# One fetch of the turned probabilities per pair of groups, a plan that counts open transfers, and two PSUM tiles for the last sums

## The chip, the cores and the metric

The kernel runs on one core of a Trainium2 chip. TensorE (PE) multiplies matrices, VectorE (DVE), ScalarE (ACT) and GpSimd (POOL) work on elements, and SyncE (SP) issues every transfer (DMA) of this kernel. The metric is the device time of one execution in microseconds (us); lower is better. The three runs of the kernel before took 588.96, 589.66 and 590.10 us, with a median of 589.66.

## The reference

An attention over four batches of eight heads and 768 positions feeds a feed-forward layer. Each query sees the keys less than 16 positions away, and beside them one summary for each of the 24 blocks of 32 keys: the block's largest key, element by element, and its mean value. All arrays are fp32.

```python
def _attn_ref(q, k, v):                       # B, H, S, D = 4, 8, 768, 64
    k_sum = k.reshape(B, H, nb, block, D).max(axis=3)        # block = 32, nb = 24
    v_sum = v.reshape(B, H, nb, block, D).mean(axis=3)
    scores_l = scale * np.matmul(q, k.transpose(0, 1, 3, 2))
    mask_l = np.abs(pos[:, None] - pos[None, :]) < window    # window = 16
    scores_s = scale * np.einsum('bhsd,bhnd->bhsn', q, k_sum) + np.log(block)
    scores_all = np.concatenate([np.where(mask_l, scores_l, -1e9), scores_s], axis=-1)
    a = softmax(scores_all)
    return np.matmul(a, np.concatenate([v, v_sum], axis=2))

x = attn_out.transpose(0, 2, 1, 3).reshape(B * S, H * D)     # 3072 x 512
out = (np.maximum(x @ w_in, 0.0) ** 2) @ w_out               # 512 -> 2048 -> 512
```

## The kernel before, in words

**Tiling.** The 3072 tokens are cut into 48 groups of 64 queries (a window of one batch, all eight heads). A window's 64 queries see 94 local keys and 24 block keys, 118 in all. Eight groups are a unit of 512 tokens, which is what the feed-forward layer works on. Every fp32 product there is made of three products of a high and a low part, so a group of six matmuls on PE (four with the high part `gh`, two with the low part `gl`, each 128x512) is the usual step. Of the six units, two are worked directly: `ffn` with the hidden product (line 1050) and the outer one (line 1074). The other four are two couples, each worked with seven products in place of eight (`first_product` line 1340, `products` line 1454, `mixed` line 1647 for the second couple's first layer with weights folded by the kernel itself). The weights `wW` come in sixteen chunks (`raw<-wW`, line 983), are split into high and low parts by ACT (line 986) and DVE (lines 989 to 1003), and stay in SBUF tiles `w...`.

**A visit.** Groups are worked in pairs. A visit of PE is the scores of one pair (line 647) followed by the values of an earlier pair (line 854). Between a pair's scores and its values lie: the mask (DVE, line 721), the exponential (ACT, line 778), the normalisation (DVE, lines 790 to 797), the turn of the probabilities from queries to keys, and the values. For the first eight groups PE turns them. From then on a group's probabilities are turned in three steps:

- T (line 826): DVE transposes each 32x32 block of a 128x512 tile into a tile `a`.
- TW (line 837): SP stores `a` in a DRAM buffer `turn`, one transfer of 256 KB.
- TR (line 841): SP fetches it back into `a` with the blocks in their new places, four transfers of 64 KB, one for each 32 partitions.

So a pair takes two stores and eight fetches. The fetches of one group wait for that group's own store.

**What sets the order.** Nothing is emitted in program order. Each piece of work is a task of the class `Plan` with an engine, an estimated cost, a sort key (mostly a due time) and the buffers that it takes and uses. `Plan.order` plays the tasks through, each engine always taking the ready task with the smallest key, and the instructions are emitted in that order. Every engine then runs its own list strictly in order: an instruction that waits holds all that are behind it on its engine. For SP this means that a load waiting for PE to free its tile holds the transfers behind it. On top of that, each transfer is given one of eight completion semaphores in turn, and waits for the transfer eight before it in SP's list. The plan before knows the rate of transfers and the engine's issue time, but not these eight. The constants at the head of the file (`VISITS`, `T0`, `STEP`, `SUMS`, `HALF_AT` and others) are the due times and leads that go into the keys.

**The tiles that the change touches.** `a` and `r`, two slots of 128x512 each, hold the turned probabilities; pairs use them in turn, except for the earliest. `turn` has four DRAM buffers of one group. In PSUM lie two double tiles `o0` and `o1` of 2x128x512, and two tiles `att0` and `att1` and two `h` of 128x512. In `products`, a couple's seven products (j from 0 to 6) are summed in PSUM, and `acc` names the tiles; products 4 and 6 share `acc[4]`, which is the double tile `o0`. The function `plus` adds such a sum to an SBUF tile on DVE (line 1400) and `leave` stores the result (line 1393). For the last product of the last couple the sum is already in two halves of 512 columns, `C12`, which both read `o0`.

## Time and profile before

| what | value |
|---|---|
| median of three runs | 589.66 us |
| profiled execution | 588.6 us |
| its span, first to last instruction or transfer | 586.8 us |
| PE busy | 573.3 us (98%) |
| DVE / ACT / POOL busy | 443.9 / 353.0 / 99.2 us |
| granted clock of PE | full throughout |
| bytes moved | 149.63 MB, mean 255 GB/s |
| SP waiting for a store `turn<-a` at a fetch | 12.0 us, 10 times |
| SP waiting for DVE at a store `turn<-a` | 20.7 us, 14 times |

Rows of a timeline read: start in us, length in us, engine, line, operation, output and input, size, and how many alike follow each other; in brackets is the engine's idle time just before and what ended it. The listed length of a matmul overlaps the next one. A row of SP is the time it took to issue, not the transfer itself. The chain of waits, followed back from the last instruction, has rows of the same kind, and there a DMA row is the time from issue to landing.

### The profile page before, as it was taken

What the parts mean: (1) busy time and instruction counts of PE and PEld (TensorE: products, weight loads), DVE (VectorE), ACT (ScalarE), POOL (GpSimd) and SP (SyncE); (2) the same over time, 40 slices, a digit from 0 to 9 for tenths busy, and PEclk for the clock granted to TensorE, in tenths of its full rate; (3) what the DMA queues carried; (4) which work ended last, traced back from release to release, by engine and by line L of the source; (5) the groups of instructions that cost most, each with busy time, mean ns of one, the idle gap of its engine ahead of it and who ended that gap; (6) DMA issues with size and microseconds to landing.
All of it is one profiled execution on the core that took longest, in us unless ns stands there. A gap on an engine that the chain in (4) does not pass through costs nothing.

```text
span 586.8 us, 12058 instructions
## 1 busy us (share of the span) xinstructions
PE 573.3 (98%) x4084; PEld 467.0 (80%) x4084; DVE 443.9 (76%) x1018; ACT 353.0 (60%) x876; POOL 99.2 (17%) x165
## 2 busy tenths in 40 slices
PE   8999999999999999999999999999999999999996
PEld 6787878777788888888778888888878888888885
DVE  5999899578457647765986877999968966769863
ACT  2999877667646646465754566676746424654442
POOL 4300005073568004420120022000000000000000
PEclk9999999999999999999999999999999999999999
DMA  8998885869998796996979945999885456667672
GB/s 313 324 394 304 304 301 161 289 214 336 356 325 261 235 332 201 322 320 185 268 248 296 363 153 183 295 303 287 271 268 178 122 158 194 197 187 232 196 225 99
DMA packets 120273, 149.63 MB, mean 255 GB/s; under 512 B 10556, under 2 KB 79164, under 8 KB 120212
## 3 DMA queue, kind: packets, MB, share of 16 engines
q1 hardware_dynamic: 120212, 148.86, 78.0%
q8 instruction: 33, 0.54, 0.4%
q14 instruction: 28, 0.23, 0.1%
HBM read 103.99 MB, written 44.04 MB: 252 GB/s over the span
## 4 chain that ended last, share of the span: by engine, by line
PE 71%; DMA 14%; DVE 5%; SPq 3%; ACT 3%; issue 2%; POOL 2%; DVEq 0%; ACTq 0%
PE o L1454 26%; PE h L1340 15%; PE o L1074 8%; PE o L1647 6%; DMA raw<-wW 6%; PE h L1050 6%; PE sz L1647 4%; PE x L854 3%; PE att L647 2%; DMA qvpa_lent<-vF 2%; DMA turn<-a 2%; DMA a<-turn 1%; PE att L1647 1%; DMA fv_lent<-vS 1%; DMA scr_i<-w 1%
## 5 line engine op out<-in xcount | busy, mean ns | idle before, releaser
L1454 PE MATMUL o<-gh,w 128*128 128x512 f32 x448 | 121.5, 393 | 0.0
L1436 ACT CAST gh<-g 128x512 fp32r<-128x512 f32 x112 | 68.5, 621 | 54.4 <-PE o L1454 25.2
L1454 PEld LDWEIGHTS o<-gh,w 128*128 128x128 f32 x448 | 83.1, 188 | 18.4 <-ACT gh L1436 0.8
L1441 DVE TENSOR_TENSOR gl<-g,gh 128x512 fp32r<-128x512 f32 x112 | 76.5, 695 | 20.9 <-ACT gh L1436 20.6
L1050 PE MATMUL h<-xh,w 128*128 128x512 f32 x240 | 75.0, 392 | 1.2 <-DVE w L1003 0.9
L1454 PE MATMUL o<-gl,w 128*128 128x512 f32 x224 | 69.5, 391 | 0.0
L1340 PE MATMUL h<-xh,w 128*128 128x512 f32 x224 | 69.1, 390 | 0.0
L1074 PE MATMUL o<-w,gh 128*128 128x512 f32 x240 | 62.2, 395 | 1.4 <-ACT gh L1061 1.2
L778 ACT ACTIVATE p<-p,small 128x118 f32<-128x118 f32 x160 | 61.0, 386 | 1.1 <-DVE small L721 0.7
L1050 PEld LDWEIGHTS h<-xh,w 128*128 128x128 f32 x240 | 44.7, 188 | 12.2 <-DVE w L1003 1.7
L1074 PEld LDWEIGHTS o<-w,gh 128*128 128x128 f32 x240 | 44.3, 188 | 11.8 <-ACT gh L1061 1.9
L1454 PEld LDWEIGHTS o<-gl,w 128*128 128x128 f32 x224 | 41.8, 188 | 9.6 <-DVE gl L1441 0.9
L1340 PEld LDWEIGHTS h<-xh,w 128*128 128x128 f32 x224 | 42.0, 188 | 9.1 <-ACT r L1350 0.4
L1050 PE MATMUL h<-xl,w 128*128 128x512 f32 x120 | 46.7, 389 | 0.0
L1340 PE MATMUL h<-xl,w 128*128 128x512 f32 x112 | 43.6, 389 | 0.0
L1350 ACT ACTIVATE r<-h 128x512 f32<-128x512 f32 x32 | 19.1, 596 | 37.1 <-PE h L1340 36.9
L660 POOL COPY kb<-kb 128x96 f32<-128x96 f32 x25 | 8.6, 343 | 193.3 <-ACT kw L672 70.9
L1064 DVE TENSOR_TENSOR gl<-r,gh 128x512 fp32r<-128x512 f32 x30 | 23.2, 774 | 20.3 <-ACT gh L1061 16.9
L721 DVE CUSTOM_DVE_ANT_0 p<-att,mask 128x118 f32<-128x118 f32 x152 | 33.1, 275 | 2.6 <-PE att L647 2.5
L1074 PE MATMUL o<-w,gl 128*128 128x512 f32 x120 | 33.6, 389 | 0.0
L1431 DVE TENSOR_TENSOR g<-g 128x512 f32<-128x512 f32 x48 | 32.8, 689 | 0.4
L778 ACT ACTIVATION_READ_ACCUMULATOR p<-p,small 128x1 f32 x160 | 30.4, 190 | 0.0
(209 smaller groups left out, 1077.7 us busy)
## 6 DMA issues: line engine op xcount, KB each, us to landing
raw<-wW SPq DMA_DIRECT2D x32, 512.0 KB
w<-scr_s SPq DMA_DIRECT2D x64, 256.0 KB
w<-scr_a SPq DMA_DIRECT2D x48, 256.0 KB
turn<-a SPq DMA_DIRECT2D x40, 256.0 KB
a<-turn SPq DMA_DIRECT2D x160, 64.0 KB
scr_t<-ci SPq DMA_DIRECT2D x32, 256.0 KB
w<-scr_i SPq DMA_DIRECT2D x32, 256.0 KB
w<-scr_t SPq DMA_DIRECT2D x32, 256.0 KB
```

The lines of the kernel that those rows point to most:

```text
L721: nc.vector.tensor_tensor_reduce(out=pr.tile[:, j, :KEYS], in0=score_at(g, 0, j), in1=mask_of(g)[0], scale=-SCALE, scalar=-NEG, op0=ALU.ad ...
L778: nc.scalar.activation(x, score_tile(g, p % parts)[:, p] if by_pe else x, AF.Exp, bias=nm.tile[:, p : p + 1], scale=SCALE if by_pe else -1 ...
L1050: nc.tensor.matmul(cut(h), lhsT=lhs.tile[:, k * P : (k + 1) * P], rhs=rhs[:, k, c0 : c0 + n], start=(i == 0), stop=(i == 3 * KT - 1),)
L1064: lambda: nc.vector.tensor_tensor(out=cut(gl), in0=cut(r), in1=cut(gh).bitcast(F32), op=ALU.subtract),
L1074: nc.tensor.matmul(o_of(o, t), lhsT=terms[i][0].tile[:, (t - t0) * P : (t - t0 + 1) * P], rhs=terms[i][1].tile, start=(first and i == 0), ...
L1340: nc.tensor.matmul(h.tile, lhsT=lhs.tile[:, k * P : (k + 1) * P], rhs=rhs[:, k, c0 : c0 + TU], start=(i == 0), stop=(i == 3 * KT - 1),)
L1350: t2 = add(f"RL{name}", "ACT", 0.56, lambda: nc.scalar.activation(r.tile, h.tile, AF.Relu), due + 2 - R_LEAD, [t1], take=[r], use=[h])
L1431: lambda x=x, ins=ins, op=op: nc.vector.tensor_tensor(out=x.tile, in0=ins[0].tile, in1=ins[1].tile, op=op),
L1436: f"GH{s}_{n}", "ACT", 0.54, lambda x=x, gh=gh: nc.scalar.copy(out=gh.tile, in_=x.tile), due - GH_LEAD, ready,
L1441: lambda x=x, gh=gh, gl=gl: nc.vector.tensor_tensor(out=gl.tile, in0=x.tile, in1=gh.tile.bitcast(F32), op=ALU.subtract),
L1454: nc.tensor.matmul(o.tile[:, d], lhsT=chunk.tile[:, w * HALF + d * P : w * HALF + (d + 1) * P], rhs=y.tile, start=begins and w == 0 and y ...
L1647: nc.tensor.matmul(o.tile, lhsT=lhs(w, k), rhs=y[k], start=begins and i == 0, stop=i == 5, skip_group_check=not begins,)
```

## The change

1. **The fetch.** The turned probabilities of a pair lie in one 128x1024 tile (one slot `a`, one slot `rr`, the same SBUF as the two of 128x512 had), and one of two DRAM buffers holds both groups of a pair. Each group is still turned and stored by itself. The fetch is a task of the pair: four transfers of 128 KB after both stores, where there were two times four of 64 KB, each four after its own store. Bytes and the 512-byte runs are the same.
2. **The plan** counts open transfers: a task says how many it issues (`issues`), and a list of the last eight landings of each queue holds an issue back until the one eight before it has landed. The assumed rate goes from 350 to 400 GB/s, and a fetch is counted as `TR_COST`.
3. **The last sums.** For the second couple, products 4 and 6 are summed in the two tiles `att0` and `att1`, held together by the small class `Banks`, and not in the double tile `o0`. The sum after product 4 (`C22`) is made in two halves.
4. **The numbers** that the plan's keys are made from are all new, so the order changes on every engine, over the whole program.

```diff
...
...
-TR_LEAD = 14
-VISITS = 52.2, 68.6, 100.8, 120.6, 146.3, 157.3, 168.5, 203.8, 235.1, 248.6, 260.4, 276.5, 297.7, 318.5, 349.1, 370.1, 390.1, 396.1, 402.1, 408.1, 416.9
+TR_COST = 1.9
+TR_LEAD = 20
+VISITS = 49.9, 82.3, 89.1, 118.5, 125.9, 145.2, 165.2, 188.4, 200.7, 237.6, 248.4, 254.4, 281.2, 289.4, 332.1, 355.6, 367.5, 379.2, 399.2, 406.4, 412.4
...
         return self.of(self.buf.tile)
 
 
+class Banks:
+
+
+    def __init__(self, bufs):
+        self.bufs = bufs
+
+    @property
+    def tile(self):
+        return self
+
+    def __getitem__(self, at):
+        d = at[1]
+        if isinstance(d, int):
+            return self.bufs[d].tile
+        assert d.stop == d.start + 1
+        return self.bufs[d.start].tile.unsqueeze(1)
+
+
-        self.take, self.use = ([getattr(b, "buf", b) for b in x] for x in (take, use))
+        self.take, self.use = ([getattr(c, "buf", c) for b in x for c in getattr(b, "bufs", (b,))] for x in (take, use))
 
 
 class Plan:
 
 
 
-    HOP, DMA_LATENCY, DMA_RATE = 0.12, 1.9, 350e3
+    HOP, DMA_LATENCY, DMA_RATE, LANES = 0.12, 1.9, 400e3, 8
 
 
 
...
     def __init__(self):
         self.tasks = []
 
-    def add(self, name, engine, cost, emit, key, after=(), take=(), use=(), size=0, begin=0.0, behind=None, late=0.0, keeps=False):
+    def add(self, name, engine, cost, emit, key, after=(), take=(), use=(), size=0, begin=0.0, behind=None, late=0.0, keeps=False, issues=1):
-        t.behind, t.late, t.keeps = behind, late, keeps
+        t.behind, t.late, t.keeps, t.issues = behind, late, keeps, issues if size else 0
         t.index = len(self.tasks)
         self.tasks.append(t)
         for b in t.take + t.use:
...
+        lanes = {}
 
...
                 t = found
                 if t is None:
                     continue
+                before = lanes.setdefault(e, [0.0] * self.LANES)
+                if t.issues and before[-self.LANES] > now:
+                    free[e] = before[-self.LANES]
+                    heapq.heappush(events, (free[e], n + 0.25, None))
+                    continue
                 tasks.remove(t)
                 for b in t.take:
                 free[e] = end = now + t.cost + self.SWITCH * (t.narrow and not narrow)
+                for i in range(1, t.issues):
+                    free[e] = end = max(end, before[i - self.LANES] + t.cost * (1 - i / t.issues))
                 if e == "PE":
                     narrow = t.narrow
                 if t.size:
                     pipe = max(pipe, end) + t.size / self.DMA_RATE
                     end = pipe + self.DMA_LATENCY + t.late
+                    before.extend([end] * t.issues)
                 t.end = end
                 n += 1
                 heapq.heappush(events, (end + self.HOP, n, t))
...
 
 
     items = [(u, f) for u in range(NU) for f in range(NF)]
-    T0, SLOW, STEP, LEAD = 28.0, 6.4, 6.2, 1.5
+    T0, SLOW, STEP, LEAD = 28.5, 6.4, 5.9, 1.5
...
         warm(i)
 
 
-    q_bufs, v_bufs, p_bufs, a_bufs = {}, {}, {}, {}
+    both_r = sb.tile([P, 2 * TU], F32, tag="rr", name="rr", bufs=1)
+    kinds["r"] = Slots(None, "r", 2, [both_r[:, k * TU : (k + 1) * TU] for k in range(2)])
+    kinds["rr"] = Slots(sb, "rr", 1)
+    kinds["a"] = Slots(sb, "a", 1)
+    q_bufs, v_bufs, p_bufs, a_bufs, both_a, both_d, t_TW = {}, {}, {}, {}, {}, {}, {}
     first_v = [x for i in range(-(-S // P // 4)) for x in lend(f"fv{i}")]
     for g in reversed(range(NG)):
         pairs = (P, NPAIR, P)
...
             q_bufs[g] = buf("q", 3, (P, NPAIR, TQ), F32, f"q{g}")
             v_bufs[g] = buf("v", NV, (P, DM), F32, f"v{g}", fixed=True)
             p_bufs[g] = buf("p", 2, pairs, F32, f"p{g}", fixed=True)
-            a_bufs[g] = buf("a" if g < APART or g // 2 % 2 == 0 else "r", 2, (P, DM), F32, f"a{g}")
+            if g % 2:
+                both_a[g // 2] = Buf(kinds["a" if g < APART or g // 2 % 2 == 0 else "rr"], (P, 2 * DM), F32, f"a{g}")
+            a_bufs[g] = Part(both_a[g // 2], g % 2 * DM, (g % 2 + 1) * DM)
 
 
     t_S, t_M, t_KC, t_T, t_V, t_XL, t_A, t_LV = ({} for _ in range(8))
...
 
             assert not early
             rest = [t_G[0, NQ - 1, k] for k in (2, 3)] if g >= APART else []
-            t_T[g] = add(f"T{g}", "DVE", 0.63, turn, due - 9, [t_n, *rest], take=[a], use=[pr])
-            d = buf("turn", 4, (NSQ, SQ, NSQ, NPAIR * SQ), F32, f"turn{g}", dr)
+            t_T[g] = add(
+                f"T{g}", "DVE", 0.63, turn, due - 9, [t_n, *rest], take=[] if g % 2 else [a], use=[pr] + [a] * (g % 2),
+                behind=t_T[g - 1] if g % 2 else None,
+            )
+            if not g % 2:
+                both_d[g // 2] = buf("turn", 2, (2, NSQ, SQ, NSQ, NPAIR * SQ), F32, f"turn{g}", dr)
+            d = both_d[g // 2]
 
             def store():
-                nc.sync.dma_start(out=d.tile.rearrange("i c j e -> (i c) (j e)"), in_=a.tile)
+                nc.sync.dma_start(out=d.tile[g % 2].rearrange("i c j e -> (i c) (j e)"), in_=a.tile)
 
             def fetch():
                 for j in range(NSQ):
                     nc.sync.dma_start(
-                        out=a.tile[j * SQ : (j + 1) * SQ].rearrange("c (i e) -> c i e", i=NSQ),
-                        in_=d.tile[:, :, j].rearrange("i c e -> c i e"),
+                        out=both_a[g // 2].tile[j * SQ : (j + 1) * SQ].rearrange("c (b e) -> c b e", e=NPAIR * SQ),
+                        in_=d.tile[:, :, :, j].rearrange("b i c e -> c (b i) e"),
                     )
 
-            t_w = add(f"TW{g}", "SP", 0.45, store, due - 8.5 - TR_LEAD, [t_T[g]], take=[d], use=[a], size=4 * P * DM, late=TURN_LATE[0])
-            t_A[g] = add(f"TR{g}", "SP", 1.75, fetch, due - 8 - TR_LEAD, [t_w], use=[a, d], size=4 * P * DM, late=TURN_LATE[1])
+            t_TW[g] = add(
+                f"TW{g}", "SP", 0.45, store, due - 8.5 - TR_LEAD, [t_T[g]], take=[] if g % 2 else [d],
+                use=[a] + [d] * (g % 2), size=4 * P * DM, late=TURN_LATE[0], behind=t_TW[g - 1] if g % 2 else None,
+            )
+            if not g % 2:
+                return
+            t_A[g - 1] = t_A[g] = add(f"TR{g}", "SP", TR_COST, fetch, due - 8 - TR_LEAD, [t_TW[g - 1], t_TW[g]], use=[a, d], size=8 * P * DM, late=TURN_LATE[1], issues=4)
 
     def values(both, x_of):
         for i, g in enumerate(both):
...
             if s:
                 sums[s][-1].update({("before", k): mixed_end[k] for k in range(2)})
         *acc, u2, u3, made = sums[s]
+        if s and len(acc) == 6:
+            acc[4:] = [Banks([Buf(kinds["atts"], None, None, f"acc{s}_{d}") for d in range(2)])]
+            sums[s] = [*acc, u2, u3, made]
         bank = acc[0], acc[1], acc[2], acc[3], acc[4], acc[3], acc[4]
 
         def by_two(x):
...
             elif j == 3:
                 last_of("w1_1", plus("U3", u3, o, u2, due, [t_p, made["U2"]], [u3]))
             elif j == 4:
-                leave(f"22_{s}", u3, 1, 1, due + 1, [plus("C22", u3, o, u3, due, [t_p, made["U3"]])])
-                made["before", 5] = [made["U3"]]
+                ds = [slice(d, d + 1) for d in range(2)] if s else [slice(0, 2)]
+                t_22 = [plus("C22", u3, o, u3, due, [t_p, made["U3"]], d=d) for d in ds]
+                leave(f"22_{s}", u3, 1, 1, due + 1, t_22)
+                made["before", 5], made["22"] = [made["U3"]], t_22
             elif j == 5:
                 x = buf("t", 3, (P, 2 * DM), F32, f"c21_{s}") if s else Buf(kinds["w1_2"], (P, 2 * DM), F32, f"c21_{s}")
                 leave(f"21_{s}", x, 1, 0, due + 1, [plus("C21", x, o, u2, due, [t_p, made["U2"]], [x])])
-                made["before", 6] = [made["C22"]]
+                made["before", 6] = made["22"]
             elif not end:
                 leave(f"12_{s}", u2, 0, 1, due + 1, [plus("C12", u2, o, u2, due, [t_p, made["C21"]])])
...
```

The parts left out give `issues` to other tasks with more than one transfer, and use the pair tiles where their SBUF is lent out after the last pair.

Three places show how the order moves (a row stands for an instruction, or for several alike). Names carry a number for the tile or the allocation.

The first is SP's list around the last pairs but one. `turn_5032` and `turn_5117` before, and `turn_4823` in the change, are the DRAM buffers of groups 44 and 45; `w_...<-scr_s` and `w_...<-scr_i` are weights of a couple, which wait for PE to be done with the tile's last ones; `v_...` are local values. Before:

```order
L837 DMA turn_5032<-a_5025 128x512
L1626 DMA w_997<-scr_i_104 128x2x256 x2
L1626 DMA w_1035<-scr_i_106 128x2x256 x2
L841 DMA a_5025<-turn_5032 32x4x128 x4
L837 DMA turn_5117<-a_5096 128x512
L599 DMA v_81<-vS 96x512
L599 DMA v_82<-vS 96x512
L1626 DMA w_911<-scr_i_108 128x2x256 x2
L841 DMA a_5096<-turn_5117 32x4x128 x4
```

In the change:

```order
L877 DMA turn_4823<-a_4820 128x512
L1470 DMA w_897<-scr_s_94 128x512
L877 DMA turn_4823<-a_4820 128x512
L633 DMA v_82<-vS 96x512
L633 DMA v_83<-vS 96x512
L1470 DMA w_921<-scr_s_95 128x512
L1441 DMA out<-u_0_4652 128x2x512
L1470 DMA w_921<-scr_s_96 128x512
L881 DMA a_4820<-turn_4823 32x8x128 x4
```

The store of the second group stands behind one weight load where four weight loads and four fetches stood, and the pair's one block of fetches stands behind three transfers of weights and output.

The second is DVE's list where the weight chunks 9 and 10 are split (between 77 and 85 us of the trace before). A chunk takes three rows, in the change at lines 1034, 1040 and 1048; its third, which makes `w9`, is what PE takes. `gl0_...` are low parts of hidden units. Before:

```order
L989 TENSOR_SCALAR raw9_977<-raw9_977 128x1024
L989 TENSOR_SCALAR raw10_1099<-raw10_1099 128x1024
L995 SCALAR_TENSOR_TENSOR t9_1130<-t9_1130,raw9_977 128x1024
L1064 TENSOR_TENSOR gl0_7_1212<-r0_7_1176,gh0_7_1190 128x512
L995 SCALAR_TENSOR_TENSOR t10_1181<-t10_1181,raw10_1099 128x1024
L1003 TENSOR_TENSOR w9_1214<-t9_1130,w9_1214 128x2x512
```

In the change:

```order
L1048 TENSOR_TENSOR w8_1132<-t8_985,w8_1132 128x2x512
L1040 SCALAR_TENSOR_TENSOR t9_1073<-t9_1073,raw9_977 128x1024
L1109 TENSOR_TENSOR gl0_6_1167<-rr_80,gh0_6_1151 128x512
L1034 TENSOR_SCALAR raw10_1048<-raw10_1048 128x1024
L1048 TENSOR_TENSOR w9_1169<-t9_1073,w9_1169 128x2x512
L1040 SCALAR_TENSOR_TENSOR t10_1125<-t10_1125,raw10_1048 128x1024
```

The second row of chunk 10 stood ahead of the third of chunk 9, and stands behind it.

The third is SP's list around the last two chunks that are loaded, 15 and 14 (between 94 and 112 us of the trace before). `v_...<-fv_w` put block means beside local values, `scr_a<-w` store weights for the couples, and the two stores `turn` are of groups 12 and 13. Before:

```order
L602 DMA v_81<-fv_w_968 24x512
L1182 DMA scr_a_96<-w_0_704 256x1x256
L1182 DMA scr_a_96<-w_1_734 256x1x256 x2
L602 DMA v_82<-fv_w_968 24x512
L983 DMA raw_1419<-wW 128x512
L602 DMA v_80<-fv_w_968 24x512
L983 DMA raw_1419<-wW 128x512
L837 DMA turn_1445<-a_1427 128x512
L837 DMA turn_1455<-a_1451 128x512
L983 DMA raw_1470<-wW 128x512 x2
L841 DMA a_1427<-turn_1445 32x4x128 x4
L841 DMA a_1451<-turn_1455 32x4x128 x4
```

In the change:

```order
L636 DMA v_82<-fv_w_1098 24x512
L1227 DMA scr_a_97<-w_0_658 256x1x256
L1227 DMA scr_a_97<-w_1_706 256x1x256 x2
L636 DMA v_83<-fv_w_1098 24x512
L636 DMA v_81<-fv_w_1098 24x512
L877 DMA turn_1383<-a_1376 128x512
L1028 DMA raw_1401<-wW 128x512 x2
L877 DMA turn_1383<-a_1376 128x512
L1028 DMA raw_1409<-wW 128x512 x2
L881 DMA a_1376<-turn_1383 32x8x128 x4
```

The two halves of chunk 15 were apart and now follow each other, behind the first of the pair's two stores. At the end of DVE's list two rows make the last sum in both versions; before, the first of them carries the wait for PE for both, and in the change each waits for its own tile.

57 lines of the change are left out of this document (29 added, 28 removed).

## The prediction

> **What bounds the kernel now.** I read the profile in this order: busy time by stretch of the span, the waits of PE, then the timelines of PE, SP and DVE around each wait, and the chain that ended last. The first view cuts the span into stretches (its first columns are length and PE busy time; the last two are DMA share and GB/s).
>
> ```profile
> 0.00:62.00 62.00, 57.29 (x705) 46.66 (x706) 53.65 (x122) 47.79 (x138) 13.06 (x54) 1.00 0.94 337
> 62.00:115.00 53.00, 50.78 (x369) 40.48 (x370) 43.32 (x86) 38.38 (x81) 7.69 (x8) 1.00 0.77 254
> 115.00:160.00 45.00, 44.50 (x302) 35.86 (x302) 30.21 (x90) 30.86 (x83) 24.17 (x28) 1.00 0.86 298
> 160.00:418.00 258.00, 258.00 (x1912) 209.98 (x1914) 193.38 (x519) 155.96 (x432) 54.29 (x75) 1.00 0.84 269
> 418.00:446.00 28.00, 26.39 (x212) 21.39 (x205) 18.98 (x46) 16.64 (x44) 0.00 (x0) 1.00 0.89 276
> 446.00:583.00 137.00, 136.38 (x602) 112.60 (x600) 103.68 (x159) 63.38 (x105) 0.00 (x0) 1.00 0.59 176
> 583.00:586.80 3.80, 0.00 (x0) 0.00 (x0) 0.70 (x2) 0.00 (x0) 0.00 (x0) 1.00 0.36 138
> ```
>
> PE bounds it: 573.34 of 586.80 us, at the full granted clock. The change adds and removes no product of matrices, so only the 13.46 us in which PE is idle can shrink: 4.71 before 62 us, 2.22 from there to 115, 0.50 to 160, none at all to 418, 1.61 to 446, and 0.62 + 3.80 at the end. The largest of PE's waits behind the start (columns: total us, times, longest):
>
> ```profile
> PE x L854 <- DMA a<-turn: 1.9, 3, 1.3
> ```
>
> These are the values of a pair, waiting for its turned probabilities. That path is what the change rebuilds.
>
> **The last two fetches (418 to 446), the largest term.** PE, then SP's queue, one row of DVE, and four links of the chain that ended last:
>
> ```profile
> 405.62 0.63 PE L647 MATMUL att<-kb,q 64*64 64x118 f32 x16
> ...
> 411.88 1.07 PE L1454 MATMUL o<-gh,w 128*128 128x512 f32 x4
> ...
> 413.24 1.07 PE L1454 MATMUL o<-gh,w 128*128 128x512 f32 x4
> ...
> 417.41 0.63 PE L647 MATMUL att<-kb,q 64*64 64x118 f32 x16
> ...
> 419.58 1.21 PE L1454 MATMUL o<-gh,w 128*128 128x512 f32 x4
> ...
> 429.37 0.69 PE L854 MATMUL x<-a,v 118*64 118x64 f32 x16
> 431.31 0.69 PE L854 MATMUL x<-a,v 118*64 118x64 f32 x16 [1.26 <-DMA a<-turn]
> ...
> 440.35 0.69 PE L854 MATMUL x<-a,v 118*64 118x64 f32 x16
> 441.39 0.69 PE L854 MATMUL x<-a,v 118*64 118x64 f32 x16 [0.36 <-DMA a<-turn]
> ```
> ```profile
> 416.78 2.63 SPq L1626 DMA_DIRECT2D w<-scr_i  x4
> 420.30 1.75 SPq L841 DMA_DIRECT2D a<-turn  x4
> 422.14 0.38 SPq L837 DMA_DIRECT2D turn<-a  x1
> ...
> 426.04 3.08 SPq L841 DMA_DIRECT2D a<-turn  x4
> ```
> ```profile
> 417.70 0.70 DVE L826 STREAM_TRANSPOSE a<-p 128x512 f32<-128x512 f32 x1
> ```
> ```profile
> 406.66 1.08 PE x L854 x32
> ...
> 422.14 3.83 DMA turn<-a
> 426.04 1.65 SPq L841
> 428.69 2.38 DMA a<-turn
> ```
>
> Group 45 was turned at 418.40, but its store was issued only at 422.14: SP stood at four weight loads, which wait for PE, and at the four fetches of group 44. The store took 3.83 us, the fetches 1.65 to issue and 2.38 to land, so the turned values came at 431.07, and PE had been ready since 429.91 (the values of two groups take 1.08 us where they don't wait, so those of one 0.54). The two stalls cost 431.31 − 429.37 − 0.54 = 1.40 and 441.39 − 440.35 − 0.54 = 0.50, 1.90 together.
>
> Now count from the start of the scores of groups 44 and 45 (405.62 before). A visit with its switch is 419.58 − 417.41 = 2.17, a group of six matmuls 413.24 − 411.88 = 1.36. In the changed order PE runs that visit, six groups, the visit of 46 and 47 (from 10.33 on), seven groups, and then wants the values of 44 and 45: 2.17 + 8.16 + 2.17 + 9.52 = 22.0 after the start (23.75 before). The store of 45 now has one weight load between it and the store of 44; that load needs the weights of the two groups before the second visit to be done, so it is free at 10.3. Turned at 418.40 − 405.62 = 12.8 as before, or up to 1.4 sooner by DVE's new order, the store is issued at 11.4 to 12.8 and has landed at 15.2 to 16.6. The four fetches now stand behind two loads of local values, two weight loads and a store of output; the weight loads wait for the two groups after the second visit, until 10.33 + 2.17 + 2.72 = 15.2. So the fetches go at 15.3 to 16.7 and land 1.65 + 2.38 later, at 19.3 to 20.7. That is 1.3 to 2.7 ahead of 22.0: the first stall should go. Twice the bytes in each of four transfers eats part of this, and would have to eat all of it.
>
> For 46 and 47 the window from scores to values grows from 440.35 − 417.41 = 22.94 (1.40 of it the other stall) to 2.17 + 9.52 + 1.2 + eleven groups of 1.36 = 27.9. DVE turns group 47 only behind the low half of the values of 44 and 45, which costs about 3 us of it, and SP holds its fetches behind two weight loads; I estimate some 2 us left over. Bounds: −1.9 (both stalls gone) to +1.4 (the first doubled, the second as it is); I take **−1.6**, near the first because both sums come out positive.
>
> **The end.** The last rows of PE, DVE and SP:
>
> ```profile
> 581.53 0.62 PE L1454 MATMUL o<-gh,w 128*128 128x512 f32 x2
> 581.99 0.39 PE L1454 MATMUL o<-gl,w 128*128 128x512 f32 x1
> 582.41 1.29 DVE L1400 TENSOR_TENSOR u<-o,u 128x512 f32<-128x512 f32 x2 [3.19 <-PE o L1454]
> 583.13 0.93 SPq L1393 DMA_DIRECT2D out<-u  x2
> ```
>
> Both halves of the last sum started after PE's very last matmul, for they read one tile. With two tiles the first half needs only the three matmuls less, those from 581.53 on: it can start about 0.65 us earlier, 0.645 being the length of one half, so the second starts where the first used to and ends one half earlier. The last store leaves some 0.6 earlier. Bounds 0 and −0.65; I take **−0.6**. The other new pair of tiles, of the product two before, has weight groups behind it and is worth nothing.
>
> **62 to 115.** Rows of DVE, PE, SP and ACT:
>
> ```profile
> 80.19 1.22 DVE L995 SCALAR_TENSOR_TENSOR t<-t,raw 128x1024 uint32<-128x1024 uint32 x1
> ```
> ```profile
> 82.59 0.50 PE L1050 MATMUL h<-xh,w 128*128 128x512 f32 x1 [0.66 <-DVE w L1003]
> ...
> 109.79 2.11 PE L1074 MATMUL o<-w,gh 128*128 128x512 f32 x8 [1.16 <-ACT gh L1061]
> ```
> ```profile
> 98.40 1.81 SPq L983 DMA_DIRECT2D raw<-wW  x1
> ...
> 101.09 0.51 SPq L983 DMA_DIRECT2D raw<-wW  x1
> ```
> ```profile
> 106.79 1.15 ACT L986 ACTIVATE t<-raw 128x1024 f32<-128x1024 f32 x1 [6.38 <-DMA raw<-wW]
> ```
>
> At 82.59 PE waits for the low part of weight chunk 9, and DVE had done the row at 80.19, which belongs to chunk 10, ahead of it; in the changed order that row stands behind. It takes 1.22 off a stall of 0.66 and the 0.16 by which a listed matmul hides idle time (0.39 listed, 0.23 from start to start in the rows of the end above): −0.8. At 109.79 the rounding of a hidden unit stood on ACT behind the first conversion of chunk 15, whose halves SP had issued 2.7 us apart, a load of local means between them. In the changed order the conversion still stands ahead of that rounding, but the halves leave together: 0.8 (the load between, from 100.2 to 101.09) to 2.7 us sooner, against a stall of 1.16 + 0.16; I take half of it, −0.7. Against both, the first visits are packed closer: the pair 8, 9 has 5.4 us less from scores to values (four groups), and can bring a wait of its own. Bounds: −2.8, the 2.22 of idle time and what four gaps hide, to +1.3, the larger stall over again. I take **−1.5**.
>
> **115 to 160.** One stall, behind eight fetches in a row:
>
> ```profile
> 148.33 5.34 SPq L841 DMA_DIRECT2D a<-turn  x8
> ```
> ```profile
> 155.31 0.69 PE L854 MATMUL x<-a,v 118*64 118x64 f32 x16 [0.33 <-DMA a<-turn]
> ```
>
> Four issues would be done some 2.6 us sooner; the stall of 0.33 should go. Bounds −0.5 and 0; I take **−0.3**.
>
> **The middle, 160 to 418**, has no idle PE to win. What it can lose: a pair's fetch now waits for both stores. The margin can be read at groups 38 and 39:
>
> ```profile
> 380.66 1.85 SPq L841 DMA_DIRECT2D a<-turn  x4
> ```
> ```profile
> 385.40 1.15 PE L854 MATMUL x<-a,v 118*64 118x64 f32 x32
> ```
>
> With the 2.38 of above the later group landed near 384.9, half a us ahead of its visit. The earlier group did not need its earlier fetch, since both halves are multiplied in one visit: what counts is the later group, which waited for its own store before too. Four issues follow that store in both versions, and in the new order these stand directly behind the stores. Fetching 128 KB by each instead of 64 makes the last land later, by at most 64 KB more times four at the stretch's 269 GB/s, 1.0 us, less the second block of four that no longer stands in SP's queue. Bounds 0 and +2; I take **+0.3**.
>
> **Before 62 us** the order is new everywhere and DVE and ACT are as full as PE; I see no reason for a sign: ±1, **0**. After 446 PE has no gap and the order is alike: 0. Eighty issues at about 0.44 us (1.75 for four) are 35 us of SP's time; none of it is PE's except where a stall above stands behind it. So it is no term of its own.
>
> **Sum.** −1.6 − 0.6 − 1.5 − 0.3 + 0.3 + 0 = −3.7. The profiled execution took 588.6 (the span and 1.8 around it), so the changed one would take 584.9. The median of the runs is 589.66, 1.06 above it; on that scale the forecast is **586.0 us**.
>
> **Rivals.**
> *Only the late gains come.* The early stretch is a chain of loads at a DMA share of 0.94 and 0.77, and one stall replaces another there. For it: the gaps before 115 us have four different releasers. Against it: both moves are in the order, and each is priced from a row. It gives −1.6 − 0.6 = −2.2, or 587.5.
> *The planned order works everywhere.* All tuned-away gaps go: 1.9 + 0.65 + 2.8 + 0.5, and some 0.9 of the head's 4.71, 6.7 in all: 583.0. For it: each gap has a mover in the new order. Against it: the same was true of the old order, which left them. The Trainium skill ("DMA: Bandwidth & Descriptors", the section "Rules for kernel authors") says to merge many small transfers, since below 64 KB one pays mostly overhead; these stood at 64 KB, and by that rule this rival would gain in weight. The rows do not bear it out as far as time goes, since the bytes and the pieces of a transfer stay.
> *The fetch of a pair is not issued in time (slower).* The fetch is one block of four behind the later store. If that store, or a load that waits for PE ahead of the block, comes late, both groups are late where only the second was, and the middle's margin is half a us. The place is the visits of 160 to 418, some fifteen pairs: at a mean of 0.5 us late each, +7.5, less the 2.2 of the late gains is +5.3; at 0.33 us, +2.8, or 592.5, which I take as its price. It decides from 0.23 us a pair. For it: the margin read above. Against it: none of these visits waits now.
> *The change's stall at 431 stays.* SP still holds the fetches of 44 and 45 behind weight loads that wait for PE. Then −0.6 − 1.5 − 0.3 + 0.3 = −2.1, or 587.6; if the early gains fail too, 589.1, no change.
>
> **How the numbers follow.** Forecast (585 to 587): 0.42. Only late gains: 0.18. All gaps: 0.14. The stall stays: 0.13, of which 0.05 with the early gains lost as well. Slower: 0.13. A difference under 0.2%, 1.2 us, can hardly be told from none. Faster by more: 0.42 + 0.18 + 0.14 + 0.08 − 0.04 for the spread of the second and fourth = 0.78; within: 0.05 + 0.04 + 0.01 = 0.10; slower: 0.12. For 8 in 10 the range leaves out the bulk of the slower rival and the far end of the gains: 582.8 to 590.0.
>
> **What would show it.** In the changed profile PE's wait for the turned probabilities should be gone from the list or under 0.5 us; the fetches of 44 and 45 should land over 1 us ahead of their visit; the first half of the last sum should start while PE still runs; the stretch from 160 to 418 should keep PE busy throughout; and PE's waits for DVE's and ACT's parts of weights and hidden units between 62 and 115 should fall by about 1.5 us. The forecast is wrong if waits for the turned probabilities appear in the middle, if a new wait before 115 is as long as those that went, or if the head grows by more than 1 us.

## The result: slower by 1.0%, against a forecast of 0.6% faster

The changed kernel took 596.24 us (median of four runs, 595.52 to 598.13) against 589.68 us before: a ratio of 1.0101, 95% interval [1.0071, 1.0132]. The forecast was 586.0 with a range to 590.0, so it was wrong in its sign. The profiled execution took 595.52 us, its span is 593.6, 6.8 above the span before. Times here and below are medians of the runs in the usual, faster state; a few runs were far slower and are left out.

The first view is again busy time by stretch of the span, of the changed kernel. The columns that count here: length, PE busy, then at the end granted clock, DMA share and GB/s.

```profile
0.00:62.00 62.00, 54.50 (x694) 44.18 (x695) 52.55 (x128) 47.02 (x140) 13.64 (x54) 1.00 0.91 324
62.00:115.00 53.00, 52.04 (x380) 42.78 (x379) 46.18 (x83) 41.58 (x84) 11.12 (x9) 1.00 0.82 286
115.00:160.00 45.00, 45.00 (x308) 36.98 (x307) 32.05 (x94) 31.10 (x85) 23.25 (x25) 1.00 0.91 318
160.00:418.00 258.00, 251.90 (x1912) 206.00 (x1911) 186.73 (x529) 152.00 (x417) 37.88 (x55) 0.99 0.81 257
418.00:446.00 28.00, 25.96 (x140) 20.94 (x139) 21.15 (x48) 15.02 (x39) 0.00 (x0) 1.00 0.95 297
446.00:583.00 137.00, 136.09 (x627) 112.83 (x628) 104.64 (x161) 66.62 (x112) 0.00 (x0) 1.00 0.61 181
```

PE's idle time fell where gains were forecast, from 2.22 to 0.96 us between 62 and 115 and from 0.50 to none up to 160. The middle, which had no idle PE at all, now has 6.10 us, and it is the only one of these stretches whose granted clock is not full. Between 418 and 446 the idle time grew from 1.61 to 2.04. The view of PE's waits (total us, times, longest) says what they are:

```profile
PE x L899 <- DVE ci L1269: 4.1, 1, 4.1
...
PE o L682 <- POOL kb L695: 1.9, 2, 1.4
...
PE x L899 <- ACT g L1727: 1.6, 1, 1.6
PE x L899 <- DMA a<-turn: 1.4, 1, 1.4
...
PE att L682 <- DMA q<-qW: 1.1, 1, 1.1
PE h L1095 <- ACT rr L1104: 1.0, 1, 1.0
PE h L1385 <- DMA w<-scr_i: 0.9, 2, 0.7
```

**One stall and its slow clock.** The largest is at a single visit, that of the values of groups 26 and 27. PE at that place:

```profile
252.60 0.64 PE L682 MATMUL att<-kb,q 64*64 64x118 f32 x16
253.05 0.58 PE L682 MATMUL att<-kw,q 64*64 64x118 f32 x16
257.70 1.98 PE L899 MATMUL x<-a,v 118*64 118x64 f32 x32 [4.06 <-DVE ci L1269]
259.61 1.22 PE L1385 MATMUL h<-xh,w 128*128 128x512 f32 x2
```

After the wait of 4.06 us the same work takes longer: the values 1.98 us, where an undisturbed visit (428.98, below) takes 1.15. The same view as above, in short windows, shows the granted clock (third column from the end):

```profile
250.00:254.00 4.00, 3.63 (x44) 2.69 (x42) 0.42 (x1) 0.60 (x1) 1.56 (x5) 1.00 1.08 379
254.00:258.00 4.00, 0.30 (x6) 0.33 (x8) 3.27 (x12) 1.91 (x4) 0.00 (x0) 0.70 0.50 108
258.00:259.00 1.00, 1.00 (x24) 1.00 (x22) 1.00 (x3) 0.86 (x2) 0.00 (x0) 0.50 0.77 235
...
262.00:263.00 1.00, 1.00 (x5) 0.82 (x4) 0.74 (x7) 1.00 (x7) 0.00 (x0) 0.80 1.02 299
```

The clock records put the half clock at 255.56 to 262.39. PE worked in 4.7 us of that, so at most 2.35 us went to the clock, on top of the wait. The account below has 6.25 us lost at this place; less the wait of 4.06 that leaves about 2.2 for the clock, and this figure is used from here on (the expectations below still reckon with 2.45).

**The whole difference.** Each product was given the time that it takes undisturbed, and these times were added up in PE's order. A product's start less this sum is PE's lag, in which the idle time that listed lengths hide is counted too. It is an estimate from the rows of both traces. The lag of the changed kernel less that of the kernel before, step by step:

```
stretch                              forecast   measured
before 62 us                             0        +1.8
62 to 160                              -1.8       -3.6
160 to 418                             +0.3       +7.6   (+6.25 at 257.7; about +1.5 at 372; about +1.4 at 389; -1.5 is what before loses there)
418 to 446                             -1.6       +0.9
more changes from visits to products     0        +0.6   (three more, 0.2 each by the account)
the end                                -0.6       -0.6
sum                                    -3.7       +6.7   (spans: +6.8)
```

### The profile page after: what moved, and what is told of

The parts are those of the page before. It is cut to its first block, busy times and chain, and to the rows that moved or that the text cites. A ratio compares the mean times of both kernels' runs of the same rounds, so it can differ in the third digit from the quotient of the medians.

```text
span 593.6 us, 11904 instructions
## 1 busy us (share of the span) xinstructions
PE 572.3 (96%) x4084; PEld 469.0 (79%) x4084; DVE 446.8 (75%) x1043; ACT 354.8 (60%) x876; POOL 85.9 (14%) x141
## 4 chain that ended last, share of the span: by engine, by line
PE 72%; DMA 12%; DVE 8%; ACT 4%; SPq 2%; issue 2%; DVEq 0%; ACTq 0%
PE o L1502 19%; PE h L1385 11%; PE o L1119 10%; PE h L1095 9%; PE o L1697 6%; DMA raw<-wW 4%; PE sz L1697 4%; PE att L1502 4%; PE x L899 3%; PE att L682 2%; DMA kb<-kT 2%; PE att L1697 2%; DMA a<-turn 1%; DVE ci L1269 1%; DMA scr_s<-cs 1%
## 5 line engine op out<-in xcount | busy, mean ns | idle before, releaser
L1502 PE MATMUL o<-gh,w 128*128 128x512 f32 x384 | 103.6, 392 | 0.0
L1502 PEld LDWEIGHTS o<-gh,w 128*128 128x128 f32 x384 | 71.5, 188 | 15.1 <-issue 0.2
L1502 PE MATMUL o<-gl,w 128*128 128x512 f32 x192 | 59.1, 389 | 0.0
L695 POOL COPY kb<-kb 128x96 f32<-128x96 f32 x25 | 10.8, 433 | 233.1 <-PE att L682 85.6
L1502 PEld LDWEIGHTS o<-gl,w 128*128 128x128 f32 x192 | 36.0, 188 | 7.6
L1109 DVE TENSOR_TENSOR gl<-rr,gh 128x512 fp32r<-128x512 f32 x30 | 23.1, 769 | 24.5 <-ACT gh L1106 24.4
L1104 ACT ACTIVATE rr<-h 128x512 f32<-128x512 f32 x30 | 17.8, 593 | 22.2 <-PE h L1095 22.1
```

The costliest lines, as they stand in the source:

```text
L1109: lambda: nc.vector.tensor_tensor(out=cut(gl), in0=cut(r), in1=cut(gh).bitcast(F32), op=ALU.subtract),
L1502: nc.tensor.matmul(o.tile[:, d], lhsT=chunk.tile[:, w * HALF + d * P : w * HALF + (d + 1) * P], rhs=y.tile, start=begins and w == 0 and y ...
```

## The experiments

What stood just ahead of the stalled visit on SP, in the changed kernel:

```profile
245.34 0.32 SPq L877 DMA_DIRECT2D turn<-a  x1
245.71 0.97 SPq L1335 DMA_DIRECT2D w<-scr_i  x2
246.78 0.42 SPq L1219 DMA_DIRECT2D scr_s<-cr  x1
247.30 0.59 SPq L1219 DMA_DIRECT2D scr_s<-cs  x1
247.94 1.65 SPq L1335 DMA_DIRECT2D w<-scr_i  x1
249.68 2.92 SPq L881 DMA_DIRECT2D a<-turn  x4
```

So between the store of group 27 and the pair's fetch the new order has three weight loads of 256 KB (PE does not wait for them here: moved behind the fetch, below, they hold nothing up there) and two stores of weight sums of 512 KB, `cr` and `cs`. Landing times, worked out from the semaphore events of the trace:

```
transfer                 issued    landed   took
turn<-a (group 27)       245.34    248.74   3.40
w<-scr_i                 245.71    251.14   5.43
w<-scr_i                 246.23    251.87   5.64
scr_s<-cr                246.78    253.22   6.44
scr_s<-cs                247.30    254.63   7.34
w<-scr_i                 247.94    255.69   7.75
a<-turn, first of four   249.68    256.05   6.37
a<-turn, last of four    252.06    257.35   5.29
```

When the fetch was issued none of the five had landed. The 1.75 MB landed between 248.74 and 255.69, which is 264 GB/s, while the DMA engines were full (a share of 1.08 from 250 to 254, above), and the last of the fetch came behind them, 7.67 us after its first issue. The values started 0.35 after its landing. The DVE adds that the view of waits names are only what ended next to it (at 257.62): in the kernel with the fetch moved ahead, below, the values run before these adds begin. The theory was then: *the fetch is late by the bytes ahead of it, and the long wait costs the clock as well.* The rivals: the group was turned or stored too late; the pair's fetch itself is to blame (four transfers of twice the size, after both stores); another wait at the same place ends as late.

**Where edits move transfers**, they move tasks in the list that the planner returns, just before the instructions are emitted: `put(names, anchor)` takes the named tasks out and puts them ahead of the anchor (behind it with a 1). `TW27` is the store of group 27, `TR27` the fetch of 26 and 27, `HL...` are weight loads of 256 KB, `QL...` loads of queries, `CL...` loads of mixed weights, `PS...` stores of output. `N27` and `T27` are the normalisation and the turn of group 27 on DVE, `SCi4_1` is a weight sum `ci` of 3.1 us there, and `WSi4_1_0` a store of 256 KB of that sum.

### Scores repeated: does the length of the wait cost the clock?

```diff
-            for g in then:
-                scores(g, range(NPAIR), False)
+            for _ in range(4 if then and then[0] == 28 else 1):
+                for g in then:
+                    scores(g, range(NPAIR), False)
```

The scores ahead of the stalled values are computed four times, which adds 2.4 us of PE work inside the wait.

> The changed kernel, with the scores of groups 28 and 29 multiplied four times in place of once (the same results written again): 3 x 0.97 = 2.9 us of needless work on PE, placed in the 4.06 us in which PE waits for the values of 26 and 27. If the long idle time is what halves PE's clock for some 6.8 us behind it (which costs 2.45 us), the clock stays full and the time falls by 2.4 us, to 593.8, although PE does more. If the clock falls for another reason, or the time was lost in the wait alone, the time stays at 596.2.

Measured: 594.86 us (10 runs), ratio 1.0048 [1.001, 1.0086]. PE's timeline at the place:

```profile
259.60 1.15 PE L899 MATMUL x<-a,v 118*64 118x64 f32 x32 [2.35 <-DVE ci L1276]
```

Added work and wait are 4.8 us, no less than the wait of 4.06, yet the values take 1.15, and the clock was full throughout this execution (mean 1.00, against 0.994). By the ratios the kernel with more work was the faster one: against 1.0101 some 3 us were regained, but the two intervals overlap. The two profiles show that the clock falls in the idle wait and stays full when the wait is filled with work. What it costs is read from the rows, about 2.2 us; the times do not contradict it, but cannot show it. In the ten runs the mean clock was between 0.988 and 1.000, so in others it fell too, at places that no profile shows.

### The fetch moved ahead

```diff
+put(['TR27'], 'TW27', 1)
```

> The changed kernel, with the fetch of groups 26 and 27 moved on SP to right behind their second store, ahead of three weight loads and the two 512 KB stores of the weight sums; nothing else moves. Theory of the backlog (the fetch was issued in time, but its bytes stood behind some 1.8 MB that were issued just ahead of it): the turned values land near 252.5 in place of 257.35, the wait of 4.06 us and the slow clock behind it go, -6.2 us, 590.0; the moved transfers come 3 to 4 us later and may cost up to 2. Theory of the pair (the fetch is late because it waits for both stores) and theory of the late turn (DVE turned group 27 too late): the store of 27 still lands at 248.7 and the fetch can go only 0.9 us earlier, so 3.2 us of wait remain, 595, or 592.5 if so short a wait leaves the clock alone.

Measured: 601.63 us, ratio 1.019 [1.0117, 1.0264]: not faster, as every theory had had it, but slower than the change by the median (the intervals overlap). PE, then DVE and ACT:

```profile
256.14 1.15 PE L899 MATMUL x<-a,v 118*64 118x64 f32 x32
263.87 1.22 PE L1385 MATMUL h<-xh,w 128*128 128x512 f32 x2 [6.58 <-ACT rr L1395]
```
```profile
259.39 0.43 DVE L1254 TENSOR_TENSOR ci<-w 128x256 f32<-128x256 f32 x1 [8.22 <-DMA scr_s<-cr]
```
```profile
261.16 0.63 ACT L1405 ACTIVATE g<-rr 128x512 f32<-128x512 f32 x1 [7.94 <-DVE ci L1254]
```

The fetch was issued at 251.95, landed at 255.92, and the values ran without a wait: the first half of the theory holds. But SP could issue it only when the store of group 27 had landed, and held the loads and the stores of `cr` and `cs` behind it. Those stores landed at 259.27 and 260.62; DVE waits for them to reuse the tiles, ACT for DVE, and PE's next hidden product for ACT to empty its PSUM tile. So two chains end at this spot, and to move the fetch only moved the lateness to the other. In the changed kernel the second chain was just as late: its rows, DVE and then ACT, end at 257.84, 0.14 after the values began.

```profile
253.41 0.42 DVE L1254 TENSOR_TENSOR ci<-w 128x256 f32<-128x256 f32 x1 [5.88 <-DMA scr_s<-cr]
254.66 1.10 DVE L1254 TENSOR_TENSOR ci<-w 128x256 f32<-128x256 f32 x3 [0.82 <-DMA scr_s<-cs]
```
```profile
257.25 0.59 ACT L1395 ACTIVATE rr<-h 128x512 f32<-128x512 f32 x1
```

### The turn moved ahead

On DVE the normalisation and the turn of group 27 go ahead of a weight sum, and on SP its store goes ahead of the store of that sum.

```diff
+put(['N27', 'T27'], 'SCi4_1')
+put(['TW27'], 'WSi4_1_0')
```

> The changed kernel, with the normalisation and the turn of group 27 moved on DVE ahead of a weight sum of 3.1 us, and its store moved on SP ahead of the store of that sum; the fetch keeps its place behind the weight transfers. Theory of the late turn: the turned values are ready 4 us earlier, the wait at 257.7 goes, -6.2 us, 590.0. Theory of the backlog: the fetch still stands behind the same weight transfers and lands at most 1 us earlier, 595; down to 592.5 if the wait gets short enough to leave the clock alone.

Measured: 599.29 us, ratio 1.0139 [1.0079, 1.02]. The store of group 27 was issued at 242.69, 2.65 sooner than in the change, and landed at 247.83, 0.91 sooner; the fetch still stood behind the same five transfers, which were themselves issued 1.9 to 2.2 later, and landed at 259.10.

```profile
259.49 1.98 PE L899 MATMUL x<-a,v 118*64 118x64 f32 x32 [5.11 <-ACT rr L1395]
```

The store came earlier and the fetch later. A late turn or a late store is not the cause.

### Fetches by group in the new order

```diff
             def store():
                 nc.sync.dma_start(out=d.tile[g % 2]..., in_=a.tile)
+                if g % 2:
+                    fetch_of(g - 1)
-            def fetch():
+            def fetch_of(x):
...
+            def fetch():
+                fetch_of(g)
```

Each group has its own four fetches of 64 KB again; the order stays that of the change.

> The changed kernel and its order, with the fetch of each pair undone: four transfers of 64 KB for the first group right behind the second group's store, and four of 64 KB for the second group where the pair's fetch stands. Theory of the pair: the first group of 26 and 27 is there in time and the second half of the bytes lands earlier, the wait at 257.7 falls to some 2 us and the clock stays, 590 to 592. Theory of the backlog: the second group's fetch stands behind the same weight transfers, the wait shrinks by the half visit of 0.54 at most, 595.5 to 596.5; 80 more issues on SP do nothing or cost up to 1 us elsewhere.

Measured: 603.95 us, ratio 1.0211 [1.0136, 1.0285]. The longest of its waits of PE:

```profile
PE x L904 <- DVE ci L1274: 4.4, 1, 4.4
```

The stall is at the same visit: the fetch of group 26 landed at 255.25, that of 27, which stood behind the five transfers, at 262.91. Fetching by the pair is not what made it; in this order four transfers are, if anything, better than eight. The time is longer than either theory had, and PE came to this visit 4.5 us later than in the change already (its scores at 257.09), for reasons that were not taken apart.

### Three weight loads moved behind the fetch

```diff
+put(['HL2_13_1', 'HL2_14_0', 'HL2_14_1'], 'TR27', 1)
```

This takes 0.75 MB from ahead of both chains. The changed kernel itself ran again beside it.

> The changed kernel, with three 256 KB weight loads (chunks 13 and 14 of the third unit, which PE wants some 25 us later) moved on SP from ahead of the fetch of groups 26 and 27 to right behind it; nothing else moves. Theory of the backlog: fetch and the two 512 KB stores of weight sums stand behind 0.75 MB less, which is 2 to 3 us at the 250 to 350 GB/s of this stretch; both land that much earlier, PE's wait falls from 4.06 to 1 to 2 us, and as it is then shorter than what lets the clock fall, the 2.45 us of the slow clock go too: -4.5 to -6, 590 to 592. If the transfers' order here does not set the end (the fetch or DVE late for another reason): within 1 us of the changed kernel.

> The changed kernel once more, so that the three below stand beside it on the same chip. Every theory: 595 to 597 against some 590 of the kernel before, with the wait at 257.7 and the slow clock behind it.

Measured on that chip: the change again 598.4 us, ratio 1.0127 [1.0065, 1.0189]; with the loads later 594.01, ratio 1.0065 [1.0035, 1.0096]. SP and PE with the loads later:

```profile
249.77 1.86 SPq L881 DMA_DIRECT2D a<-turn  x4
251.67 1.40 SPq L1335 DMA_DIRECT2D w<-scr_i  x3
```
```profile
255.10 1.15 PE L899 MATMUL x<-a,v 118*64 118x64 f32 x32 [0.33 <-DVE ci L1269]
```

The fetch landed at 254.97, 5.20 after its issue instead of 7.67, `cs` at 252.57, 4.15 after its issue instead of 7.34. The visit waits 0.33 us instead of 4.06, and the next hidden product follows it without a wait. So at this visit the bytes ahead are the cause, and both chains are cured at once where no byte is in front that is not wanted yet. By the medians 4.4 us come back, though the two intervals overlap. The change that ran beside it waits 2.90 us at this visit, with no half clock behind it, so the visit gives 2.6 of the 4.4 in these two profiles, and the rest stays open. Other waits stay as they were or vary: 2.82 at the values of 46 and 47 in this execution.

### The pair's fetch and the tiles in the old order

```diff
...
+        todo.sort(key=lambda t: places[t.name][t.at])
```

Here `places` is the order of the kernel before, written into the kernel as a list of task names. The first kernel takes the pair's fetch alone in this order (the fetch where the later group's was), the second the two PSUM tiles for the last sums as well.

> The kernel before with only the fetch of a pair: pair tiles, two stores, then four transfers of 128 KB at the place of the second group's four; every engine keeps the order of the kernel before, and the old planner numbers and the double tile of the last sums stay. Theory of the pair (the slower rival of the prediction: a fetch that waits for both stores is late): new waits for the turned probabilities in the middle, 592 or more. Theory of the order (the fetch itself is harmless, the new order lost the time): within 1.2 us of the kernel before, a little faster if anything, since the stall at 155 us was behind eight fetches (-0.5) and SP has 80 issues fewer.

> The kernel before with both mechanisms of the change and no new order: the pair's fetch (as in pair_old_order) and the two PSUM tiles for products 4 and 6 of the last couple. Theory: the mechanisms are small gains and the order lost the time: the pair's fetch 0.5 to 1, the tail 0.6, so 588.5 to 589.3 where the kernel before takes 590.4 (ratio 0.996 to 0.998). If the two PSUM tiles hinder the products beside them, 590 or more.

Measured: 589.51 us, ratio 0.9972 [0.9949, 0.9995], and 588.57, ratio 0.9975 [0.9952, 0.9999], beside kernels before of 590.41 and 589.88 (these medians alone are 0.15% and 0.22% apart). So these parts of the change are no loss, but a small gain of at most some 0.3%; the two kernels cannot be told apart by their times. The loss is in the order. The pair's fetch is not free of waits for all that: in the profile of the first kernel two visits of the middle wait for it, 0.35 us and this one, the visit of groups 38 and 39:

```profile
388.29 1.15 PE L967 MATMUL x<-a,v 118*64 118x64 f32 x32 [0.96 <-DMA a<-turn]
```

### The other transfers out of the way

```diff
 put(['HL2_13_1', 'HL2_14_0', 'HL2_14_1'], 'TR27', 1)
+put(['PS22_0'], 'TR45', 1)
+put(['PS21_0', 'PS12_0'], 'TR47', 1)
+put(['HL3_15_0', 'HL3_15_1'], 'QL41')
+put(['QL43', 'QL44'], 'CL0_23')
```

Stores of output behind the last two fetches, weight loads ahead of loads of queries for the waits at 372 and 389.

> The changed kernel with the moves of loads_later, and more on SP alone: three stores of output that nobody waits for behind the fetches of 44/45 and of 46/47; two weight loads that PE waited 0.9 us for ahead of two loads of queries; two loads of queries that PE waited 1.1 us for ahead of eight weight loads. Theory of the backlog: beside the 4.5 to 6 us of loads_later the waits at 429 (1.4), 447 (1.6), 372 (0.9) and 389 (1.1) shrink or go, -2 to -4 more: 587 to 589.5, below the kernel before. If these waits come from issue or from DVE and not from what stands ahead in the transfers: no more than loads_later.

Measured: 591.12 us, ratio 1.002 [0.9995, 1.0045]. That is above what was expected. The waits at 372, 389, 429 and 447 are gone, the visit of 26 and 27 waits 1.0 us, and a new and longer wait came, SP's and PE's rows:

```profile
375.14 0.83 SPq L622 DMA_DIRECT2D q<-qW  x2
376.03 4.80 SPq L1470 DMA_DIRECT2D w<-scr_s  x8
```
```profile
374.90 0.58 PE L682 MATMUL att<-kw,q 64*64 64x118 f32 x16
...
380.25 2.04 PE L1502 MATMUL o<-gh,w 128*128 128x512 f32 x4 [3.13 <-DMA w<-scr_s]
```

The two loads of queries wait for PE to read the tiles they overwrite (the scores of 374.45 to 375.1); moved up to that point they held eight weight loads. The last edit was too much, so it was cut back:

```diff
-put(['QL43', 'QL44'], 'CL0_23')
+put(['QL43', 'QL44'], 'CL0_31')
```

> The kernel of 'cleared' with one move put right: the two loads of queries go ahead of the last three of the eight weight loads only, not ahead of all eight (where they waited for PE and held the first of these loads, which cost PE 3.1 us). Theory of the backlog: that wait and the slow clock near it go, the other places stay cleared: 4 to 5 us below 'cleared', 585.5 to 588, faster than the kernel before by 2 to 5. If the place was not made by these loads: 590 to 591 as 'cleared'.

Measured: 587.97 us (12 runs) against 589.88, ratio 0.9972 [0.9948, 0.9995]: it beats the kernel before by a little, and the changed kernel by 1.5% (1.0127 on that chip). The middle and the last two fetches in the first view:

```profile
160.00:418.00 258.00, 256.58 (x1942) 209.74 (x1941) 192.88 (x542) 156.20 (x426) 38.61 (x55) 1.00 0.84 266
418.00:446.00 28.00, 28.00 (x178) 22.89 (x177) 20.89 (x46) 17.50 (x43) 0.00 (x0) 1.00 0.81 261
```

The span is 584.1, and against the changed kernel nothing differs but the places of some transfers in SP's list. The middle still has 1.42 us of idle PE, 0.7 of it at the values of 26 and 27. Yet the same gain was to be had in the old order (0.9975): the new numbers earn nothing that can be measured here.

### Two of the planner's constants

```diff
-    HOP, DMA_LATENCY, DMA_RATE, LANES = 0.12, 1.9, 400e3, 8
+    HOP, DMA_LATENCY, DMA_RATE, LANES = 0.12, 1.9, 400e3, 1000
```

and, in the other kernel, `DMA_RATE` 375e3 with 8 lanes. The first plan no longer counts open transfers, the second reckons a rate nearer to the measured ones (257 to 324 GB/s in the stretches of the first view up to 446).

> The changed kernel with the plan not counting open transfers (1000 allowed in place of 8); all numbers of the change stay, so the plan draws another order for the whole program. If the count itself made the order bad: below 593. If the numbers were fitted to the count, and the plan is told less of the queue: 596 or more, with stalls in other places than 257 us. Either way the first 60 us, where few transfers are open, should look as in the changed kernel.

> The changed kernel with the plan's assumed transfer rate at 375 instead of 400 GB/s (the kernel before: 350); the plan draws another order. If the assumed rate is what packs fetches too close behind other transfers: the fetches of 26/27 and 44/45 get more room and the time falls to 590 to 594. If the order is only one draw among many, of which small causes decide: anywhere between 590 and 600, with stalls at other visits.

Measured: without the count 594.65 us, ratio 1.0071 [1.0039, 1.0103], between the two values expected, and no wait at that visit; at 375 GB/s 602.32, ratio 1.0206 [1.0165, 1.0246], above all that was expected:

```profile
258.63 1.98 PE L899 MATMUL x<-a,v 118*64 118x64 f32 x32 [11.85 <-ACT rr L1395]
```

There the fetch of 26 and 27 had landed at 248.49. What came late was the other chain: the store `cr` landed at 256.73, and DVE, ACT and PE follow it at 256.81, 257.32 and 258.63.

Each constant gives another order with stalls of its own, the rate of 375 the worst of them. Each is one order out of many: they show that a better rate does not by itself place the transfers well; which part of the planner would, was not tried.

## Why the prediction was wrong

*The middle, +0.3: the step that failed.* It priced only the pair's wait for its later store, and took the margin from one pair, 38 and 39. What decides is what SP issues between that store and the fetch; in the new order that was 1.75 MB at one pair, and it cost 6.25 us: 4.06 of wait and about 2.2 of slow clock. The bounds of 0 and +2 had no row of a fetch behind large transfers in them, and the clock had no term at all. The margin was misread as well: the fetch of 39 landed at 385.53 before, 4.87 after its first issue, and not near 384.9, and its values are the second half of the visit, from about 385.94 on. That 0.4 was left, and not half a us, is near by luck. What was priced is small: the pair's fetch in the old order waits 0.96 there. That the middle had no idle PE to win was read as little to lose, but the order is new there too, and the waits at 372 (weights) and 389 (queries) came from the same cause: both went when the transfers ahead were moved.

*418 to 446, −1.6: it came out at +0.9.* The forecast had the store of 45 issued 11.4 to 12.8 us after the scores of its pair and landed at 15.2 to 16.6, the fetch issued from 15.3 to 16.7 on, and the values wanted at 22.0. In the changed kernel, SP:

```profile
417.42 0.34 SPq L877 DMA_DIRECT2D turn<-a  x1
...
419.91 0.46 SPq L1441 DMA_DIRECT2D out<-u  x1
420.83 0.33 SPq L1470 DMA_DIRECT2D w<-scr_s  x1
421.74 2.01 SPq L881 DMA_DIRECT2D a<-turn  x4
```
```profile
428.98 1.15 PE L899 MATMUL x<-a,v 118*64 118x64 f32 x32 [1.38 <-DMA a<-turn]
```

The scores were at 405.30: issued at 12.1, landed (421.68) at 16.4, fetched from 16.4 on, wanted at 22.3, all as forecast. Only the landing was at 23.55 (428.85) and not at 19.3 to 20.7: the fetch took 7.11, where 4.03 had been reckoned. One us of this was a slip in reading: 1.65 in the chain is the issue of the first of the four transfers alone; the last was issued 2.65 after it, and from first issue to last landing that fetch took 5.03 (426.04 to 431.07). The rest is that the 2.38 belongs to its last 64 KB, issued when most of what stood ahead had drained (the two weight loads ahead landed at 429.39 and 430.32), and here the fetch has twice the bytes, and a store of 512 KB (landed 425.36) and a weight load (426.46) came just before it. The same held at 46 and 47, behind two stores of output; with the three stores later both waits were gone (the two kernels of cleared transfers).

*62 to 160, −1.8 together: right in sign, small in size.* It measured −3.6; the waits at 82.59 and 109.79 and that at 155.31 are gone, as reckoned, and one of 0.96 at 112 came. That it is twice the forecast may in part be lag of the later head made good again, and is then luck. *Before 62, 0 ± 1: +1.8.* PE's waits for POOL's key sums grew from 0.5 to 1.9 us and those for DVE's normalised tiles from 0.3 to 1.6, the largest parts; no run took this apart, and it stays open why the new order is later there. *The end, −0.6: right.* The last rows of the changed kernel:

```profile
588.93 0.62 PE L1502 MATMUL att<-gh,w 128*128 128x512 f32 x2
589.13 1.37 DVE L1448 TENSOR_TENSOR u<-att,u 128x512 f32<-128x512 f32 x2 [2.50 <-PE att L1502]
589.38 0.39 PE L1502 MATMUL att<-gl,w 128*128 128x512 f32 x1
```

The first half starts at 589.13, 0.64 before PE's last product ends, and from PE's end to the span's there are 3.83 us instead of 4.42.

*The rivals.* The slower one named the side and the place, with 592.5; its mechanism, every pair a little late because the fetch is not issued in time, is refuted by the stalled fetch itself, issued 0.94 after its store had landed, by the pair's fetch in the old order (0.9972, two visits late) and by the fetches by group in the new one, which are worse. So that it named the side was luck. That the stall at 431 stays came true, and for another reason than SP held by loads that wait for PE: the fetch was issued in time. Of the signs that the prediction set against itself two came: waits for the turned probabilities in the middle, and a head longer by more than 1 us.

## What to carry to other kernels

Price a fetch by the bytes issued ahead of it at the measured rate, not by the latency of the last piece of another fetch, and look at every place where a new order puts large transfers before one that is waited for soon. To move the waited-for transfer up only shifts the lateness to those behind it that are wanted as soon; what helps is to move back what is wanted late, and not to move up what itself waits. A wait that leaves PE nearly idle for some 2 us or more can bring a stretch of half clock, and its price should be added.

## What was not expected of the hardware

**The transfers of one queue share one backlog.** From issue to landing the pair's fetch of 512 KB took 5.13 us on average over 20 pairs and 7.67 and 7.11 at the two where large transfers were just ahead. The plan's own terms give 5.3 for a fetch with nothing ahead of it (1.9 to issue, 1.3 for the bytes at 400 GB/s, 1.9 and 0.2 behind them), which is near the mean and not near the two worst; what the plan reckoned at these two places is not on record. The Trainium skill ("DMA: Bandwidth & Descriptors", the section on the anatomy of one DMA) gives about 2.0 us and the bytes at 436 GB/s for one transfer issued by GpSimd, 3.2 us for 512 KB as an estimate. SP's fetch took longer even with nothing ahead (251.95 to 255.92 in the kernel with the fetch moved ahead, 3.97), with four issues of 0.45 in it. Neither figure tells what a queue in use takes; the measurement decides.

**The clock falls after short waits.** In the profile of the change the half clock began 1.9 us into the wait of 4.06 (PE was idle from 253.64, the clock fell at 255.56). Beside it, half clock followed waits of 3.09, 2.16 and 1.73 us in the second run of the change, and not one of 2.90 us. Two windows of that run, at the wait of 1.73 and behind it:

```profile
388.00:390.40 2.40, 0.71 (x17) 0.41 (x16) 2.37 (x6) 1.64 (x7) 0.00 (x0) 1.00 1.08 272
...
391.40:394.80 3.40, 3.40 (x10) 2.65 (x9) 1.25 (x4) 1.09 (x3) 0.27 (x1) 0.52 0.77 236
```

So the length of the wait alone does not decide. The stretches of half clock lasted 3.41 us, 6.83 in the profile of the change, and 10.24 and 13.65 around the longer waits with the fetch moved ahead and at 375 GB/s: whole multiples. The Trainium skill ("TensorE: Matmul & The Clock Gate", part 1, on the clock gate) has the clock at half after an idle window of about 3.4 us and full again after a busy one, in a window that runs freely; the length of the stretches agrees. The idle times before the fall are shorter here than such a window, 1.73 and 1.9 us among them, and the measurement decides; where the windows lie, and how much idle time in one is enough, no run here tested.
